# A pruned matmul's opening: the hand-written order of its first products, transposes and pruning steps

## Chip, cores and metric

The kernel runs on one core of one Trainium2 chip. The metric is the device time of one execution in microseconds (us). The engines of the core are TensorE (PE in the profile; PEld is its weight load), VectorE (DVE), ScalarE (ACT), GpSimd (POOL) and SyncE (SP), which issues DMAs. Every time below is from a run, the page of one profiled execution, or an answer of its trace.

## The reference

x is 16 x 512 rows of 1024 numbers, w is 1024 x 1024, b has 1024, all bf16. In every column of w, each four consecutive rows form a group, and the two smaller of the four by absolute value are set to zero; then the product and the bias follow.

```
wg = w.reshape(G, M, D)                 # M = 4, G = 256
mag = jnp.abs(wg)
thr = the third of the four magnitudes in ascending order
mask = mag >= thr
wp = (wg * mask).reshape(D, D)
out = einsum("bsd,df->bsf", x, wp) + b
```

## The kernel before, in words

The 8192 rows of x are 64 token tiles of 128. TensorE multiplies a transposed tile of x (128 x 128, loaded as weights) by a stretch of the pruned weights wp, up to 512 columns wide, into a PSUM bank. For nearly the whole run (`nat`, line 241, products on line 243) it uses wp_nat, the pruned weights in the natural order of rows, and tiles of x that a DMA has transposed; there are eight products per tile and half of the columns.

**The opening** is there because at the start neither the pruned weights nor transposed tiles exist. w comes in six *pieces* (line 135): pieces 0 to 3 are 256 columns each of the first half of the rows (group block g = 0), pieces 4 and 5 are 512 columns each of the second half. Seven tiles of x (0 to 6), called packed, are loaded as they are, transposed on TensorE against an identity (`transpose`, line 194, four transposes a tile into one bank) and copied to SBUF by ScalarE (`copy_xt`, line 202). In w as loaded, each partition holds a whole group of four rows: these four *rows* are named u, v, s and t (slices 0 to 3; line 209), x is u and v, y is s and t. With them a product needs no rearranged weights: TensorE can start on a piece's row as soon as VectorE has pruned it. Seven tiles, four pieces and four rows give 112 products of 256 columns (`mm_piece`, line 215; the product is on line 229).

**Pruning a piece** (`Piece.do`, line 169) is a chain on VectorE: abs; hi and lo (maximum and minimum of the pairs); t1 and t2 (minimum of the his, maximum of the los); thr; mask; mult, which writes wp. thr and all in front of it work on all four rows, mask and mult may be cut by rows. Piece 0 has its abs cut in two (a, b), since its two halves arrive by two DMAs.

**The sums of the opening.** PSUM has eight banks for this kernel: two in the pool psum_t, for transposed tiles, and six in psum_o, for sums (lines 60 and 61). A sum takes a bank of 512 columns for two tiles and one piece (the pairs are tiles 3 and 4, 0 and 1, 2 and 5) or, for tile 6 alone, for two pieces. Tile 4 is transposed into a bank of psum_o, and the fillers write to one. When all products of a sum are done, ScalarE copies it out (`stage`, line 260) and its bank comes free for the next tile that asks.

**The orders.** What each engine does in the opening, and in which order, is written out by hand in the table `order` from line 267 on, one list of tokens for each engine; an engine takes its list strictly in order. `needs` (line 305) only says when a token may be written into the program, `emit` (line 345) writes it; the waits come from the data. Tokens:

- T5a: transpose tile 5. C5a: its copy on ScalarE. F4: four filler products of 128 columns on constants (line 143), which compute nothing.
- M5.0t: products of tile 5, piece 0, row t. x and y stand for two products.
- hi0, mask0t, mult0t and so on: steps of pruning piece 0; abs3 in ScalarE's list is the abs of piece 3.
- S3b0: copy out the sum of pair 3 and piece 0 (pair 0 is tiles 3 and 4, pair 2 is 0 and 1, pair 3 is 2 and 5). U6h0: the same for tile 6, first half of the columns.
- W0.0: DMAs (four, on SyncE; W1.0q on ScalarE) that spread the pruned weights of block 0, columns 0 to 511, from wp to wp_nat. Z, X1, Y0, Y1: further loads.
- E0, A0h0 and so on: first products from wp_nat. E0 is the first of them.

Ahead of the lists stand 6 fillers of 512 columns and 14 of 128. After the lists come the closing products of the first twelve tiles, and then seven batches of tiles with eight products for each half of the columns. Bias additions on the way out are on VectorE (lines 428 and 430).

Of the kernel before, what the change touches and what calls it, by code (L numbers as in the profile page):

```python
# [10 lines left out]
def kernel(  # L11
# [8 lines left out]
    P = 128  # L20
    bf16 = mybir.dt.bfloat16
    fp32 = mybir.dt.float32
# [10 lines left out]
    FH = 512  # L33
# [26 lines left out]
    psum_t = ctx.enter_context(tc.tile_pool(name="psum_t", bufs=2, space=bass.MemoryType.PSUM))  # L60
    psum_o = ctx.enter_context(tc.tile_pool(name="psum_o", bufs=6, space=bass.MemoryType.PSUM))
# [10 lines left out]
    def pe(i):  # L72
        return seq("pe", i)
# [7 lines left out]
    def sp(i):  # L81
        return seq("sp", i)
# [19 lines left out]
    def load_w(g, c0, c1, ma=0, mb=4, eng="sp"):  # L102
        issue(eng, w_sb[:, g, ma:mb, c0:c1], wv[:, g, ma:mb, c0:c1])
# [10 lines left out]
    def load_lead(g):  # L114
        t0 = NPK - g
        sp(nc.sync.dma_start_transpose(out=xlead[:, 4 * g:4 * g + 4, (t0 - SOLO) * P:],
                                       in_=xf[t0 * P:(NPK + LEAD) * P, g * HK:(g + 1) * HK]))
        return {t: xlead[:, :, (t - SOLO) * P:(t - SOLO + 1) * P] for t in range(t0, NPK + LEAD)}
# [22 lines left out]
    def filler(n, rep=1):  # L141
        for _ in range(n):
            pe(nc.tensor.matmul(warm_ps[:, :rep * P], lhsT=nc.const_aps.tensor(1.0, [P, P], bf16),  # L143
                                rhs=nc.const_aps.tensor(1.0, [P, rep * P], bf16), start=True, stop=True))
# [4 lines left out]
    def spread(g, c0, c1, ks=range(4), eng="sp"):  # L149
        for k in ks:  # L150
            issue(eng, wp_nat[:, 4 * g + k, c0:c1], wp[32 * k:32 * k + 32, g, :, c0:c1])
# [38 lines left out]
                self.tt(wp[:, self.g, ms, self.c0:self.c1], self.w[:, ms, :], self.mag[:, ms, :], Alu.mult)  # L190

    xpk = {}

    def transpose(t):
        xg = x_sb[t].rearrange("p (q m) -> p m q", m=4)
        bank = psum_o.tile([P, FH], fp32, name="ps") if t == 4 else psum_t.tile([P, FH], fp32, name="tp")
        tp = bank[:].bitcast(bf16)[:, :FH].rearrange("p (m q) -> p m q", m=4)
        for m in range(4):
            pe(nc.tensor.transpose(tp[:, m, :], xg[:, m, :], ident[:]))  # L199
        xpk[t] = tp  # L200
# [33 lines left out]
    def load_low(u):  # L234
        a, b_ = GROUPS[u]
        xlow = const.tile([P, 4, (b_ - a) * P], bf16, name=f"xlow{u}")
        sp(nc.sync.dma_start_transpose(out=xlow[:], in_=xf[a * P:b_ * P, HK:]))
        xq = xlow[:].rearrange("p k (q t) -> p k q t", t=b_ - a)
        return {a + t: xq[:, :, :, t] for t in range(b_ - a)}
# [20 lines left out]
    def stage(key):  # L260
        solo = key[1] == "h"
        q, h, at = (pair_of[key[0]], key[2], int(key[0] != SOLO)) if solo else (key[0], key[1] // 2, key[1] % 2)
        if (q, h) not in staged:
# [2 lines left out]

    order = {
# [7 lines left out]
        ),  # L275
        "dve": (
# [4 lines left out]
        ),  # L281
        "act": (
            "C5a C3a C4a C6a C2a C0a C1a S3b0 S2b0 abs3 S0b0 U6h0 S3b1 S0b1 S2b1 S3b2 S0b2 S2b2 S2b3 S0b3 U6h1 "
            "S3b3 U7h0 W1.0q U7h1"
        ),
        "sp": (
            "W0.0 Z W0.1 X1 W1.0p Y1 Y0 W1.1"
# [1 line left out]
    }  # L289
    written = {"X0"}  # L290
    p = {}
    halves = {0: tuple("uvst"), 1: ('x', 'y'), 2: ('u', 'v', 'y'), 3: ('x', 'y')}

    by_rows = {0}

    def all_of(tok, i):
        return [tok + x for x in halves.get(i, ("",))]

    def split_tok(tok):
        k = tok[-1] if tok[-1] in "xyabuvst" else ""  # L300
        return (tok[:-1] if k else tok), k

    transposed = []

    def needs(eng, tok):
        base, k = split_tok(tok)
        if tok[0] == "C":
            return ["T" + tok[1:]]
        if tok[0] == "T":
            return ["C" + transposed[-2]] if tok != "T4a" and len(transposed) > 1 else []  # L310
        if tok[0] == "F":
            return []
        if tok[0] == "W":
            g, h = map(int, tok[1:4].split("."))
            return [n for i, pc in enumerate(pieces) if pc[0] == g and pc[1] // FH == h for n in all_of(f"mult{i}", i)]
        if tok[0] in "XYZ":
            return []
        if tok[0] == "A":
            return ["X0", f"W0.{tok.split('h')[1]}"] + ([f"U{NPK}h{tok[-1]}"] if tok[1] == "3" else [])
        if tok[0] == "E":  # L320
            return ["X0", f"W0.{tok[1]}"]
        if tok[0] == "U":
            t, h = map(int, tok[1:].split("h"))
            if t == NPK:
                return [f"E{h}"]
            return [f"M{t}.{x}" for i, pc in enumerate(pieces) if pc[0] == 0 and pc[1] // FH == h for x in all_of(str(i), i)]
        if base[0] == "M":
            t, i = base[1:].split(".")
            return [f"C{t}a", f"mult{i}{k}"]
        if tok[0] == "S":  # L330
            q, n = map(int, tok[1:].split("b"))
            return [f"M{t}.{x}" for i, pc in enumerate(pieces) if pc[0] == 0 and pc[1] // CW == n
                    for t in pairs[q] for x in all_of(str(i), i)]
        i, step = base[-1], base[:-1]
        before = {"abs": [], "hi": ["abs"], "lo": ["abs"], "t1": ["hi"], "t2": ["lo"],
                  "thr": ["t1", "t2"], "mask": ["thr", "hi", "lo"], "mult": ["mask"]}[step]
        out_ = []
        for b_ in before:
            if b_ in ("abs", "hi", "lo") and int(i) in by_rows:
                out_ += [b_ + i + k] if step in ("hi", "lo") else [b_ + i + s for s in "ab"]  # L340
            else:
                out_.append(b_ + i + (k if b_ == "mask" else ""))
        return out_

    def emit(eng, tok):
        base, k = split_tok(tok)
        if tok[0] == "T":
            transpose(int(tok[1:-1]))
            if tok != "T4a":
                transposed.append(tok[1:])  # L350
        elif tok[0] == "F":
            filler(int(tok[1:]))
        elif tok[0] == "W":
            g, h = map(int, tok[1:4].split("."))
            spread(g, h * FH, (h + 1) * FH, {"": range(4), "p": range(2), "q": range(2, 4)}[tok[4:]], eng)
        elif tok[0] == "Z":
            load_w(1, 512, 1024)
            sp(nc.sync.dma_start(bias_sb[:], b.partition_broadcast(P)))
        elif tok[0] == "X":
            xnat.update(load_lead(int(tok[1:])))  # L360
        elif tok[0] == "Y":
            xnat.update(load_low(int(tok[1:])))
        elif tok[0] == "E":
            open_solo(int(tok[1:]))
        elif tok[0] == "U":
            t, h = map(int, tok[1:].split("h"))
            stage((t, "h", h))
        elif tok[0] == "A":
            open_nat(*map(int, tok[1:].split("h")))
        elif tok[0] == "C":  # L370
            copy_xt(int(tok[1:-1]))
        elif tok[0] == "M":
            mm_piece(*map(int, base[1:].split(".")), part[k])
        elif tok[0] == "S":
            stage(tuple(map(int, tok[1:].split("b"))))
        else:
            i = int(base[-1])
            if i not in p:
                p[i] = Piece(i)
            if eng == "act":  # L380
                p[i].abs_act()
            else:
                p[i].do(base[:-1], part[k], half.get(k, slice(0, 2)))
# [82 lines left out]
    for bi, (tb, nb) in enumerate(batches):  # L466
        if bi:
            load_batch(bi + 1)
        for j in range(nb):
            t = tb + j  # L470
            xt = xnat[t]
            o = outp.tile([P, Dout], bf16, name="o")
            if t == NT - 1:
                for n, (c0, c1) in enumerate(((0, FH), (FH, FH + CW), (FH + CW, Dout - P), (Dout - P, Dout))):
                    ps = psum_o.tile([P, FH], fp32, name="ps")
# [44 lines left out]
```

## Time and profile before

| what | value |
|---|---|
| median of the runs | 233.09 us (3 runs, 232.59 to 233.63) |
| span of the profiled execution, first to last instruction | 232.0 us |
| TensorE busy | 226.2 us, 98% of the span, 1128 products and transposes |
| VectorE busy | 107.9 us (47%) |
| ScalarE busy | 13.3 us (6%) |
| bytes moved by the DMA engines | 38.19 MB, mean 165 GB/s over the span |
| small products of the opening (line 229) | 112, 273 ns each by the profile |
| transposes (line 199) | 28 |
| fillers (line 143) | 24 |

The runs were timed apart from the profile; the profiled execution's own time is its span and what lies around it, and the span is 1.1 us under the median of the runs. A row of a timeline gives start, length, engine, line, operation, output <- input, shape and a count of merged instructions, and in brackets how long the engine sat idle ahead of it and for whom. Products on TensorE are pipelined: the length of one is longer than the distance to the next, so distances are read from the starts.

### The profile page before, as it was taken

Reading aid. Unit: us, or ns where it says so; the run is one execution under the profiler, and the core shown is the slowest. Engines: PE = TensorE matmul, PEld = TensorE weight load, DVE = VectorE, ACT = ScalarE, POOL = GpSimd, SP = SyncE. Lnnn points to the kernel's source line nnn. Section 1 sums busy time; section 2 is a strip of 40 time slices with the busy share of each in tenths; the row PEclk is TensorE's granted clock in tenths of the full one; section 3 lists DMA queues with packets and bytes.
Section 4 is the critical chain, followed back from the end, with each engine's and each line's share of the span. In section 5 each row is a group of like instructions: output and inputs, shape, how many; then the busy total and the mean of one; then the engine's idle time right before and its main releaser. Section 6 shows DMA issues by size and latency. Waiting matters only on the chain.

```text
span 232.0 us, 2815 instructions
## 1 busy us (share of the span) xinstructions
PE 226.2 (98%) x1128; PEld 110.4 (48%) x1148; DVE 107.9 (47%) x194; ACT 13.3 (6%) x26; POOL 17.6 (8%) x15
## 2 busy tenths in 40 slices
PE   7899999999999999999999999999999999999995
PEld 4786444444444444444444444444444444444443
DVE  4899967754234334334324324424424423423434
ACT  2576100000000000000000000000000000000000
POOL 1000099800000000000000000000000000000000
PEclk9999999999999999999999999999999999999999
DMA  6999999997299321991239721797229952122122
GB/s 201 255 193 266 261 182 230 277 312 271 95 206 259 123 93 54 261 273 45 93 103 275 210 90 51 146 240 212 81 90 184 241 163 77 61 90 90 48 90 90
DMA packets 79292, 38.19 MB, mean 165 GB/s; under 512 B 64176, under 2 KB 71728, under 8 KB 79280
## 3 DMA queue, kind: packets, MB, share of 16 engines
q1 hardware_dynamic: 68352, 20.75, 43.5%
q10 hardware_dynamic: 10928, 17.27, 21.1%
q8 instruction: 9, 0.15, 0.3%
q14 instruction: 3, 0.02, 0.0%
HBM read 3.28 MB, written 16.78 MB: 86 GB/s over the span
## 4 chain that ended last, share of the span: by engine, by line
PE 96%; DMA 2%; issue 1%; ACTq 0%; DVE 0%
PE ps L243 87%; PE ps L229 5%; PE tp L243 2%; DMA x<-in_x_dram 2%; PE tp L199 1%; ACTq L100 0%; DVE o L428 0%; PE ps L143 0%
## 5 line engine op out<-in xcount | busy, mean ns | idle before, releaser
L243 PE MATMUL ps<-wp_nat,xb 128*128 128x512 bf16 (+1 forms) x831 | 178.9, 375 | 0.9
L243 PEld LDWEIGHTS <-xb 128*128 128x128 bf16 x848 | 82.4, 98 | 97.5
L428 DVE TENSOR_TENSOR o<-ps,bias_sb 128x512 bf16<-128x512 f32 (+1 forms) x112 | 71.6, 677 | 113.8 <-PE ps L243 111.5
L424 POOL TENSOR_TENSOR st<-st,bias_sb 128x1024 f32<-128x1024 f32 x8 | 16.7, 2124 | 0.0
L243 PE MATMUL ps<-wp_nat,xlead 128*128 128x512 bf16 x63 | 14.7, 379 | 0.1
L243 PEld LDWEIGHTS <-xlead 128*128 128x128 bf16 x88 | 8.6, 98 | 10.2
L229 PE MATMUL ps<-wp,xt 128*128 128x256 bf16 x112 | 12.9, 273 | 0.0
L430 DVE TENSOR_TENSOR o<-ps,st 128x512 bf16<-128x512 f32 x16 | 11.1, 692 | 2.8 <-PE ps L243 2.2
L229 PEld LDWEIGHTS <-xt 128*128 128x128 bf16 x112 | 10.8, 98 | 1.2
L243 PE MATMUL ps<-wp_nat,xlow 128*128 128x512 bf16 x47 | 10.6, 379 | 0.1
L265 ACT COPY st<-ps 128x512 f32<-128x512 f32 x14 | 7.4, 594 | 3.0 <-PE ps L229 3.0
L243 PEld LDWEIGHTS <-xlow 128*128 128x128 bf16 x48 | 5.0, 103 | 5.4
L164 DVE TENSOR_TENSOR wp<-w_sb,mag 128x256 bf16<-128x256 bf16 (+2 forms) x13 | 6.2, 482 | 0.1
L164 DVE TENSOR_TENSOR mag<-mag,hi 128x256 bf16<-128x256 bf16 (+2 forms) x13 | 6.0, 482 | 0.2
L243 PE MATMUL tp<-wp_nat,xlead 128*128 128x512 bf16 x23 | 5.8, 379 | 0.0
L143 PE MATMUL ps<-const-bfloat16-1.0 128*128 128x128 bf16 (+1 forms) x24 | 4.1, 334 | 0.8 <-PEq L504 0.8
L174 DVE TENSOR_SCALAR mag<-w_sb 128x512 uint16<-128x512 uint16 (+2 forms) x6 | 2.7, 468 | 4.2 <-DMA w_sb<-in_w_dram 4.2
L199 PE MATMUL tp<-ident,x 128*128 128x128 bf16 x24 | 2.2, 224 | 1.3 <-DMA x<-in_x_dram 1.3
L143 PEld LDWEIGHTS <-const-bfloat16-1.0 128*128 128x128 bf16 x24 | 2.1, 118 | 2.4 <-issue 2.4
L164 DVE TENSOR_TENSOR hi<-mag 128x512 bf16<-128x512 bf16 (+2 forms) x7 | 3.2, 456 | 0.0
L164 DVE TENSOR_TENSOR lo<-mag 128x512 bf16<-128x512 bf16 (+2 forms) x7 | 3.1, 457 | 0.0
L199 PEld LDWEIGHTS <-x 128*128 128x128 bf16 x28 | 1.8, 115 | 2.0 <-DMA x<-in_x_dram 2.0
(18 smaller groups left out, 15.0 us busy)
## 6 DMA issues: line engine op xcount, KB each, us to landing
out_dram<-o ACTq DMA_DIRECT2D x58, 256.0 KB, 2.4
wp_nat<-wp SPq DMA_DIRECT2D x14, 128.0 KB, 3.3
out_dram<-o ACTq DMA_DIRECT2D x10, 128.0 KB, 1.7
w_sb<-in_w_dram SPq DMA_DIRECT2D x2, 512.0 KB, 5.3
w_sb<-in_w_dram SPq DMA_DIRECT2D x3, 256.0 KB, 5.9
x<-in_x_dram SPq DMA_DIRECT2D x2, 256.0 KB, 4.7
x<-in_x_dram ACTq DMA_DIRECT2D x2, 128.0 KB, 4.3
bias_sb<-in_b_dram SPq DMA_DIRECT2D x1, 256.0 KB, 4.7
```

What stands on the lines that cost most here:

```text
L143: pe(nc.tensor.matmul(warm_ps[:, :rep * P], lhsT=nc.const_aps.tensor(1.0, [P, P], bf16), rhs=nc.const_aps.tensor(1.0, [P, rep * P], bf16), ...
L164: dve(nc.vector.tensor_tensor(out, a, b_, op=op))
L174: dve(nc.vector.tensor_single_scalar(self.mag[:, ms, :].bitcast(u16), self.w[:, ms, :].bitcast(u16), 0x7FFF, op=Alu.bitwise_and))
L199: pe(nc.tensor.transpose(tp[:, m, :], xg[:, m, :], ident[:]))
L229: pe(nc.tensor.matmul(ps[:, c0 + d:c1 + d], lhsT=xpk[t][:, m, :], rhs=wp[:, g, m, c0:c1], start=(new and m == ms.start), stop=(left[key] = ...
L243: pe(nc.tensor.matmul(ps, lhsT=xt[:, kt - koff, :], rhs=wp_nat[:, kt, c0:c1], start=(kt == first), stop=(kt == last)))
L265: act(nc.scalar.copy(staged[(q, h)][:, at, :, :].rearrange("p t c -> p (t c)"), ps_open.pop(key)[:]))
L424: pool(nc.gpsimd.tensor_tensor(st[:], st[:], bias.to_broadcast([P, 2, 2, CW]), op=Alu.add))
L428: dve(nc.vector.tensor_tensor(o[:, c0:c1], ps, bias_sb[:, c0:c1], op=Alu.add))
L430: dve(nc.vector.tensor_tensor(o[:, c0:c1].rearrange("p (n c) -> p n c", n=2), ps.rearrange("p (n c) -> p n c", n=2), add, op=Alu.add))
```

## The change

Only the tables of the opening change, and the few lines that know their names.

- **TensorE.** T6a moves behind the products M5.0t and M5.0s. The fillers F4 are gone. Each tile then runs its rows of piece 0 together (t, s, then u, v), and of the other pieces all seven tiles run one row before the next: t, s, x for piece 1, with the tiles in the order 3, 4, 6, 5, 2, 0, 1.
- **Tile 1** is transposed into a bank of psum_o, as tile 4 was (OWN).
- **VectorE.** hi0 and lo0 run over all four rows at once (512 columns) instead of in halves, lo first. mask0v and mult0v move ahead of abs1, as does mult0u. Piece 1 is masked as t, s, x instead of y, x. abs2 leaves its list.
- **ScalarE.** abs2 joins its list, ahead of the first copy of a sum (S0b0, then S3b0, S2b0, abs3); the later copies come in the order of the new products.
- SyncE's list is unchanged.

```diff
+    OWN = (4, 1)
...
-        bank = psum_o.tile([P, FH], fp32, name="ps") if t == 4 else psum_t.tile([P, FH], fp32, name="tp")
+        bank = psum_o.tile([P, FH], fp32, name="ps") if t in OWN else psum_t.tile([P, FH], fp32, name="tp")
...
         "pe": (
-            "T5a T3a T4a T6a F4 M5.0t M3.0t M5.0s M3.0s M4.0t M4.0s T2a M6.0s M3.0u M6.0u M5.0u T0a M4.0u T1a "
-            "M2.0s M2.0t M2.0u M6.0t M0.0u M0.0s M0.0t M1.0t M0.0v M2.0v M1.0v M5.0v M6.0v M3.0v M4.0v M1.0u "
-            "M1.0s M2.1y M3.1y M5.1y M2.1x M6.1y M0.1x M1.1x M4.1x M6.1x M5.1x M0.1y M4.1y M3.1x M1.1y M2.2y "
-            "M3.2y M1.2y M6.2y M4.2y M4.2v M5.2y M5.2v M1.2v M2.2u M0.2v M0.2y M4.2u M0.2u M5.2u M6.2v M2.2v "
-            "M3.2u M1.2u M6.3x M0.3x M5.3x M3.2v M3.3x M1.3y M4.3y M1.3x M0.3y M4.3x M3.3y M6.3y M6.2u M2.3y "
-            "M2.3x M5.3y E0 A0h0 A2h0 A1h0 A3h0 E1 A2h1 A0h1 A1h1 A3h1"
+            "T5a T3a T4a M5.0t M5.0s T6a M3.0t M3.0s M4.0t M4.0s M6.0t M6.0s M5.0u M5.0v M3.0u M3.0v T2a M4.0u "
+            "M4.0v M6.0u M6.0v T0a T1a M2.0t M2.0s M2.0u M2.0v M0.0t M0.0s M0.0u M0.0v M1.0t M1.0s M1.0u M1.0v "
+            "M3.1t M4.1t M6.1t M5.1t M2.1t M0.1t M1.1t M3.1s M4.1s M6.1s M5.1s M2.1s M0.1s M1.1s M3.1x M4.1x "
+            "M6.1x M5.1x M2.1x M0.1x M1.1x M3.2y M4.2y M6.2y M5.2y M2.2y M0.2y M1.2y M3.2v M4.2v M6.2v M5.2v "
+            "M2.2v M0.2v M1.2v M3.2u M4.2u M6.2u M5.2u M2.2u M0.2u M1.2u M3.3x M4.3x M6.3x M5.3x M2.3x M0.3x "
+            "M1.3x M3.3y M4.3y M6.3y M5.3y M2.3y M0.3y M1.3y E0 A0h0 A2h0 A1h0 A3h0 E1 A2h1 A0h1 A1h1 A3h1"
         ),
         "dve": (
-            "abs0a abs0b hi0a lo0a lo0b hi0b t20 t10 thr0 mask0t mask0s mult0t mult0s mask0u abs1 mult0u hi1 lo1 "
-            "t11 t21 mask0v thr1 mult0v mask1y mask1x mult1y abs2 mult1x lo2 hi2 t22 t12 thr2 mask2y mask2v "
-            "mult2y mask2u mult2v hi3 lo3 t13 t23 mult2u thr3 mask3x mult3x mask3y mult3y abs4 hi4 lo4 t24 t14 "
-            "thr4 mask4 mult4 abs5 lo5 hi5 t25 t15 thr5 mask5 mult5"
+            "abs0a abs0b lo0 hi0 t20 t10 thr0 mask0t mask0s mult0t mult0s mask0u mask0v mult0u mult0v abs1 hi1 "
+            "lo1 t11 t21 thr1 mask1t mask1s mult1t mask1x mult1s mult1x lo2 hi2 t22 t12 thr2 mask2y mask2v mult2y "
+            "mask2u mult2v hi3 lo3 t13 t23 mult2u thr3 mask3x mult3x mask3y mult3y abs4 hi4 lo4 t24 t14 thr4 "
+            "mask4 mult4 abs5 lo5 hi5 t25 t15 thr5 mask5 mult5"
         ),
         "act": (
-            "C5a C3a C4a C6a C2a C0a C1a S3b0 S2b0 abs3 S0b0 U6h0 S3b1 S0b1 S2b1 S3b2 S0b2 S2b2 S2b3 S0b3 U6h1 "
-            "S3b3 U7h0 W1.0q U7h1"
+            "C5a C3a C4a C6a C2a C0a C1a abs2 S0b0 S3b0 S2b0 abs3 S0b1 U6h0 S3b1 S2b1 S0b2 S3b2 S2b2 S0b3 U6h1 "
+            "S3b3 S2b3 U7h0 W1.0q U7h1"
...
-    halves = {0: tuple("uvst"), 1: ('x', 'y'), 2: ('u', 'v', 'y'), 3: ('x', 'y')}
+    halves = {0: tuple("uvst"), 1: ('s', 't', 'x'), 2: ('u', 'v', 'y'), 3: ('x', 'y')}
...
-            return ["C" + transposed[-2]] if tok != "T4a" and len(transposed) > 1 else []
+            return ["C" + transposed[-2]] if int(tok[1:-1]) not in OWN and len(transposed) > 1 else []
...
-            if b_ in ("abs", "hi", "lo") and int(i) in by_rows:
-                out_ += [b_ + i + k] if step in ("hi", "lo") else [b_ + i + s for s in "ab"]
+            if b_ == "abs" and int(i) in by_rows:
+                out_ += [b_ + i + s for s in "ab"]
...
-            if tok != "T4a":
+            if int(tok[1:-1]) not in OWN:
```

## The prediction

> **What bounds the kernel now.** I read the page's chain first, then the list of waits, then the timeline of the opening engine by engine. The first fence has the page's span, its chain by engine and by line, and the costliest group; the second the list of TensorE's waits from 6.6 us to the end.
>
> ```profile
> span 232.0 us, 2815 instructions
> ...
> PE 96%; DMA 2%; issue 1%; ACTq 0%; DVE 0%
> PE ps L243 87%; PE ps L229 5%; PE tp L243 2%; DMA x<-in_x_dram 2%; PE tp L199 1%; ACTq L100 0%; DVE o L428 0%; PE ps L143 0%
> ...
> L243 PE MATMUL ps<-wp_nat,xb 128*128 128x512 bf16 (+1 forms) x831 | 178.9, 375 | 0.9
> ```
> ```profile
> PE tp L199 <- DMA x<-in_x_dram: 0.6, 1, 0.6
> ```
>
> The chain is TensorE for 96% of the span. The one listed wait of TensorE is for x at 6.6 us, the very start of that stretch; after it TensorE is fed to the end. So the change can only act where its order differs: from the first transpose to E0, the first product that reads the pruned weights from wp_nat. What E0 gains or loses there moves the end by the same amount, as long as later data keep their lead. The opening on TensorE:
>
> ```profile
> 5.57 0.39 PE L199 MATMUL ps<-ident,x 128*128 128x128 bf16 x4
> 6.60 0.41 PE L199 MATMUL tp<-ident,x 128*128 128x128 bf16 x4 [0.64 <-DMA x<-in_x_dram]
> 6.85 0.39 PE L143 MATMUL ps<-const-bfloat16-1.0 128*128 128x128 bf16 x4
> 7.08 0.82 PE L229 MATMUL ps<-wp,xt 128*128 128x256 bf16 x6
> 7.81 0.41 PE L199 MATMUL tp<-ident,x 128*128 128x128 bf16 x4
> 8.07 0.60 PE L229 MATMUL ps<-wp,xt 128*128 128x256 bf16 x4
> 8.59 0.42 PE L199 MATMUL tp<-ident,x 128*128 128x128 bf16 x4
> 8.85 0.27 PE L229 MATMUL ps<-wp,xt 128*128 128x256 bf16 x1
> 8.96 0.39 PE L199 MATMUL tp<-ident,x 128*128 128x128 bf16 x4
> 9.18 11.19 PE L229 MATMUL ps<-wp,xt 128*128 128x256 bf16 x101
> 20.20 1.03 PE L243 MATMUL tp<-wp_nat,xlead 128*128 128x512 bf16 x4
> ```
>
> The rows are start, length, engine, line. T4's transposes end at 5.57 + 0.39 = 5.96, T6 starts at 6.60 when its x lands, F4 (four fillers) takes 6.85 to 7.08, and the last 101 of the 112 small products run from 9.18 to E0 at 20.20: 11.02 / 101 = 0.109 us each, with no gap. A transposed tile costs 0.22 (8.96 to 9.18), and 0.26 where TensorE had to wait (7.81 to 8.07), so a restart costs 0.04.
>
> **The change part by part.** First VectorE, whose rows set when weights are ready:
>
> ```profile
> 3.31 0.51 DVE L174 TENSOR_SCALAR mag<-w_sb 128x512 uint16<-128x512 uint16 x2 [3.31 <-DMA w_sb<-in_w_dram]
> ...
> 4.54 0.28 DVE L164 TENSOR_TENSOR lo<-lo 128x256 bf16<-128x256 bf16 x1
> 4.75 0.28 DVE L164 TENSOR_TENSOR hi<-hi 128x256 bf16<-128x256 bf16 x1
> 5.07 0.29 DVE L164 TENSOR_TENSOR hi<-hi,lo 128x256 bf16<-128x256 bf16 x1
> 5.39 0.49 DVE L164 TENSOR_TENSOR mag<-mag,hi 128x256 bf16<-128x256 bf16 x2
> 5.80 0.49 DVE L164 TENSOR_TENSOR wp<-w_sb,mag 128x256 bf16<-128x256 bf16 x2
> ...
> 7.43 0.43 DVE L174 TENSOR_SCALAR mag<-w_sb 128x1024 uint16<-128x1024 uint16 x1 [0.94 <-DMA w_sb<-in_w_dram]
> ...
> 7.97 0.42 DVE L164 TENSOR_TENSOR hi<-mag 128x512 bf16<-128x512 bf16 x1
> 8.31 0.42 DVE L164 TENSOR_TENSOR lo<-mag 128x512 bf16<-128x512 bf16 x1
> ...
> 11.33 0.42 DVE L164 TENSOR_TENSOR lo<-mag 128x512 bf16<-128x512 bf16 x1
> ...
> 13.39 0.42 DVE L164 TENSOR_TENSOR wp<-w_sb,mag 128x512 bf16<-128x512 bf16 x1
> ...
> 16.18 0.43 DVE L164 TENSOR_TENSOR wp<-w_sb,mag 128x512 bf16<-128x512 bf16 x1
> ```
>
> Independent steps follow each other after 0.20 (256 wide, 4.54 to 4.75) or 0.34 (512 wide, 7.97 to 8.31); a dependent one starts 0.03 after its source ends (5.07 + 0.29 = 5.36, next 5.39).
>
> *Wider first steps.* Four steps of 0.20 become two of 0.34, 0.12 less. But lo0 needs both halves of abs0, which end at 3.31 + 0.51 = 3.82: lo0 3.86, hi0 4.20, t20 4.54, t10 waits for hi0 (4.62) and starts at 4.73, thr0 5.04, mask0t 5.36 against 5.39. So the wait eats nearly all: 0.03 is left. mult0t ends at about 6.06, mult0s at 6.26, mult0u and mult0v by 7.07, all before the DMA of piece 1 lets abs1 start at 7.43.
>
> *Tile 5 ahead of tile 6.* M5.0t starts 0.04 after mult0t (the lag of the copy behind T6: 6.60 + 0.41 = 7.01, copy at 7.05 in the next fence), at 6.10; M5.0s at 6.30, done at 6.41, before x of tile 6 is there. Two products leave the bound stretch: 2 x 0.109 = **-0.22**. Cover gone (mult0s over 0.19 later), it costs one for one.
>
> *No F4*: 7.08 - 6.85 = **-0.23**. *T2 and T0* each waited shortly for x: 7.08 + 6 x 0.109 = 7.73 against 7.81, and 8.07 + 0.44 = 8.51 against 8.59, each with a restart: 2 x (0.08 + 0.04), or **-0.23** before rounding. Below they come later than their data.
>
> *M6.0t.* With F4 gone, M3 and M4 (four products) run 6.85 to 7.29, but tile 6's copy ends at 7.42. ScalarE's rows:
>
> ```profile
> 7.05 0.37 ACT L204 COPY xt<-tp 128x256 f32<-128x256 f32 x1 [0.57 <-PE tp L199]
> ...
> 9.05 0.70 ACT L204 COPY xt<-tp 128x256 f32<-128x256 f32 x2 [0.41 <-PE tp L199]
> 10.69 1.13 ACT L265 COPY st<-ps 128x512 f32<-128x512 f32 x2 [0.94 <-PE ps L229]
> 11.72 1.06 ACT L167 ACTIVATE mag<-w_sb 128x1024 bf16<-128x1024 bf16 x1
> 12.68 2.09 ACT L265 COPY st<-ps 128x512 f32<-128x512 f32 x4
> ```
>
> M6.0t starts at 7.46: a new wait of 0.17 and a restart, **+0.21**; all behind it on TensorE waits too. Then six products to 8.16 (restart counted), T2 to 8.38, four products to 8.82, T0 to 9.04, T1 to 9.26 (with its own bank of psum_o it no longer waits for the copy of tile 2), twelve products to 10.57. Piece 1's t row: abs1 ends 7.86, hi1 7.89, lo1 8.23, t21 8.77, thr1 9.08, mask1t 9.40, mult1t about 9.81 to 10.09. In time, by 0.48.
>
> *The bank wait.* In the new order the sums of piece 1 open while those of piece 0 are all open: tiles 2/5, 3/4, 6 and 0/1 hold four of psum_o's six banks, M3.1t and M5.1t take the other two. M0.1t, the sixth product of piece 1, due at 10.57 + 5 x 0.109 = 11.11, needs a seventh. It must wait for the first staging copy, S0b0, and abs2 now stands ahead of that on ScalarE. Tile 0's copy starts 0.04 after T0 ends (8.82 + 0.39 = 9.21), at 9.25; tile 1's 0.33 later (0.70 - 0.37) at 9.58, abs2 at 9.91, S0b0 0.96 later (11.72 to 12.68) at 10.87, and with the 0.59 of such a copy (1.13 for two that start 0.54 apart) it ends at 11.46. M0.1t starts at 11.50: 0.39 and a restart, **+0.43**. Behind it on TensorE stand all other products, E0 among them; ScalarE's later copies wait for those products, VectorE doesn't. The trace of before shows no wait for a bank. Its ends: nothing, if a bank came free otherwise; 1.5, if the bank given were that of the third copy (2 x 0.54 later). I take 0.43, since six open sums can be counted and ScalarE's rows are at hand.
>
> The other 79 products follow: 11.54 + 79 x 0.109 = 20.15 for E0, against 20.20. As a sum: -0.22 - 0.23 - 0.23 + 0.21 + 0.43 = **-0.04**.
>
> *abs2 moved to ScalarE, the fixed row order, the rest of VectorE.* abs2 leaves VectorE (0.34) and ends at 10.97; lo2 starts at about 11.01 instead of 11.33. So everything behind is about 0.32 early: piece 2's first weights end at 13.81 - 0.32 = 13.49, needed when 56 products are left (20.15 - 6.10 = 14.05); piece 3's at 16.61 - 0.32 = 16.29, needed at 14.05 + 28 x 0.109 = 17.10. The later banks have slack of about 0.4 or more by the same spacing. These edits cost nothing while these leads of 0.5 and 0.8 last; beyond them, one for one.
>
> *DMAs and queues.* No moved step issues a DMA, and SyncE's list is the same. Its rows, and one issue alone, that of piece 2 of the weights, with its time to landing at the end:
>
> ```profile
> w_sb<-in_w_dram SPq DMA_DIRECT2D x1, 256.0 KB, 5.9
> ```
> ```profile
> 3.59 2.02 SPq L100 DMA_DIRECT2D w_sb<-in_w_dram  x3
> 5.65 6.19 SPq L116 DMA_TRANSPOSE xlead<-in_x_dram  x1
> 11.96 3.42 SPq L100 DMA_DIRECT2D wp_nat<-wp  x4
> ```
>
> The spread of the first half (W0.0) goes out right behind the long transposing load, at 11.96, whether piece 1 is done at 11.4 or 11.0: no gain, no loss. All later transfers are asked for at the same time or earlier.
>
> So E0 moves by -0.04 us, the span to 231.96, and the median, 1.1 above the span of the profiled execution, from 233.09 to **233.05**. The end of the time outside the span has no row, and I leave it as it is.
>
> **The rivals.**
>
> *No new waits* (12%): if S0b0 is through in time (abs2 short, or another bank free), the 0.43 goes: 232.6; with M6.0t's 0.21 too, 232.4, the most that the edits can bring (0.68). For it: ScalarE stood idle 0.94 before 10.69. Against it: in the new order abs2 fills just that idle time.
>
> *The staging queue tied to a DMA* (slower, 8%): abs2 waits for piece 2 of the weights, and S0b0, so M0.1t, stands behind it. Issued at 3.59, landed 5.9 later, at 9.5, against abs2's turn at 9.91. From a landing after 9.9 on, each 0.1 us later is 0.1 us on TensorE; at 11.1 (7.5 us to landing) the time is 234.3. Against it: 5.9 here, and no row of before shows piece 2 late. With a bank that comes with the third copy, 1.1 more on TensorE, the time is 234.1 (5%).
>
> *The clock* (slower, 2%): the fillers are what keeps TensorE's clock up, and F4 goes. The first two rows are weight loads of the wide fillers at the start; the third is the stretch 6.60 to 9.18 with its granted clock in the third column from the end.
>
> ```profile
> 1.58 0.15 PEld L143 LDWEIGHTS <-const-bfloat16-1.0 128*128 128x128 bf16 x1 [0.27 <-issue]
> 2.01 0.15 PEld L143 LDWEIGHTS <-const-bfloat16-1.0 128*128 128x128 bf16 x1 [0.28 <-issue]
> 6.60:9.18 2.58, 2.58 (x32) 2.11 (x32) 1.75 (x7) 0.88 (x3) 0.00 (x0) 1.00 1.12 318
> ```
>
> A wide filler took 0.43 (1.58 to 2.01) at first, where 512-wide products later take 178.9 / 831 = 0.215: half pace. Each us at half pace costs 0.5; it decides from 2.4 us on, and 3 us of it would give 234.5. In before the stretch holds 1.00, and in the new order TensorE's idle time before 6.60 gets shorter, not longer. The Trainium skill (TensorE: Matmul & The Clock Gate, "Part 4: PE-mode transpose") says that transposes do not count as busy for the gate, which speaks against dropping F4. Its Part 1 wants a whole idle window of about 3.4 us; the trace agrees so far, in that the clock held at 1.00.
>
> **How the numbers follow.** About 0.5% (1.17 us) is what a measurement of this kernel can tell from no change. Forecast with its small errors 67%; no new waits 12%; the DMA case 8%, half of it under 0.5%; third copy's bank 5%, just within 0.5%; clock 2%; what I have not seen 6%, half to each side. The forecast's bounds are 232.4 (all gains, no wait) and about 233.9 (some leads of 0.4 to 0.5 lost); with the scatter of the runs of before, 232.59 to 233.63, the range is 232.3 to 234.0. Faster by over 0.5% needs more than the whole 0.68 and gets half of the unseen, 3%; slower gets half of the DMA case, the clock and the other half of the unseen, 4 + 2 + 3 = 9%; within, 88%.
>
> **What would show it.** Right: two 256-wide products before T6's transposes; a TensorE gap of about 0.2 after four products behind T6, and one of about 0.4 at the 34th small product, ended by a ScalarE copy; E0 near 20.15; mask0t near 5.36. Wrong: no such gap (232.6), a gap of over a microsecond, a wait of TensorE behind E0, or products farther apart than 0.109.

## The result and the profile after

The changed kernel takes 233.45 us (median of 22 runs, 233.32 to 233.65), the kernel before 233.03 (22 runs, 232.59 to 233.74): a ratio of 1.0018, 95% interval 1.0012 to 1.0025. That is 0.42 us slower, inside the predicted range and inside 0.5%, but with the other sign than the forecast of -0.04. And the changed kernel scatters by 0.33 us, the kernel before by 1.15.

The page of the changed kernel: its span, and its chain by engine and by line (lines are one higher than before).

```profile
span 231.5 us, 2828 instructions
...
PE 95%; DVE 1%; DMA 1%; ACT 1%; issue 0%
PE ps L244 88%; PE ps L230 5%; PE tp L244 2%; DMA w_sb<-in_w_dram 1%; ACT mag L167 0%; DVE hi L164 0%; PE tp L200 0%; ACT xt L205 0%; DVE lo L164 0%; DVE mag L174 0%; DVE mag L164 0%; ACT st L266 0%; DVE o L429 0%; DVE wp L164 0%
```

Two things are to be seen. The chain no longer begins with x of tile 6: it begins with the first load of w, runs through VectorE's first steps (hi, lo, mag, wp) and later through ScalarE (xt, mag, st). And the span of this execution is shorter than that of before (231.5 against 232.0), although the kernel is slower. This execution took 233.33 in all, so 1.8 us lie around the span. The profiled execution of before, at a span of 232.0, then took about 233.8: 0.8 above its own median. The prediction had read an execution from the upper end of the scatter. E0 gives the same: in 14 of the 17 profiled executions whose own time is known, the time is E0 plus 213.57 to 213.61 us (in the other three plus 213.69 to 213.81), and 20.20 + 213.6 is 233.8.

TensorE's opening in the changed kernel, as in the prediction's fence of before:

```profile
5.35 0.39 PE L200 MATMUL ps<-ident,x 128*128 128x128 bf16 x4
6.10 0.47 PE L230 MATMUL ps<-wp,xt 128*128 128x256 bf16 x2 [0.37 <-DVE wp L164]
6.41 0.38 PE L200 MATMUL tp<-ident,x 128*128 128x128 bf16 x4
6.63 1.46 PE L230 MATMUL ps<-wp,xt 128*128 128x256 bf16 x10
7.93 0.39 PE L200 MATMUL tp<-ident,x 128*128 128x128 bf16 x4
8.15 0.60 PE L230 MATMUL ps<-wp,xt 128*128 128x256 bf16 x4
8.59 0.39 PE L200 MATMUL tp<-ident,x 128*128 128x128 bf16 x4
8.81 0.39 PE L200 MATMUL ps<-ident,x 128*128 128x128 bf16 x4
9.03 10.89 PE L230 MATMUL ps<-wp,xt 128*128 128x256 bf16 x96
19.76 1.03 PE L244 MATMUL tp<-wp_nat,xlead 128*128 128x512 bf16 x4
```

T6 starts at 6.41 and waits for no DMA; it stands behind M5.0t and M5.0s, which wait for VectorE, with TensorE idle before 6.10. How early its x was there is in the DMA view of that one issue, whose last number is the time to landing, first in the changed kernel, then in the execution of before that the prediction read:

```profile
x<-in_x_dram ACTq DMA_DIRECT2D x1, 128.0 KB, 3.6
```
```profile
x<-in_x_dram ACTq DMA_DIRECT2D x1, 128.0 KB, 4.8
```

Issued at 1.8 in both, it landed at 5.4 here and at 6.6 there. T6 needs one thing more, the bank of tile 5, which is free when tile 5's copy ends (in two runs below, in which T6 does not wait for its own x, it starts 0.05 behind that copy: 5.91 behind 5.86, 5.92 behind 5.87). Here that copy runs from 5.32 to 5.69. So T6 could have started at about 5.7, in time in which TensorE now does nothing.

The two waits that the prediction added are both there. The chain of the changed kernel, start, length, what:

```profile
6.79 0.44 PE ps L230 x4
...
7.26 0.83 PE ps L230 x6
...
9.01 0.65 ACT xt L205 x2
9.66 0.96 ACT mag L167
10.61 0.48 ACT st L266
11.10 0.04 issue
11.14 8.78 PE ps L230 x79
```

M6.0t starts at 7.26 instead of 6.63 + 4 x 0.109 = 7.07, 0.19 late. The last 79 products hang on tile 1's copy, abs2 and S0b0 on ScalarE, as forecast, and begin at 11.14. The row of 96 in the timeline takes 19.76 - 9.03 = 10.73, where 96 x 0.109 is 10.47: the bank wait is 0.25.

### The profile page after: what moved, and what is told of

Its sections match the earlier page's. It is cut to its first block, busy times and chain, and to the rows that moved or that the text cites. A ratio compares the mean times of both kernels' runs of the same rounds, so it can differ in the third digit from the quotient of the medians.

```text
span 231.5 us, 2828 instructions
## 1 busy us (share of the span) xinstructions
PE 227.6 (98%) x1144; PEld 110.7 (48%) x1144; DVE 107.9 (47%) x193; ACT 13.8 (6%) x27; POOL 17.6 (8%) x15
## 3 DMA queue, kind: packets, MB, share of 16 engines
HBM read 3.28 MB, written 16.78 MB: 87 GB/s over the span
## 4 chain that ended last, share of the span: by engine, by line
PE 95%; DVE 1%; DMA 1%; ACT 1%; issue 0%
PE ps L244 88%; PE ps L230 5%; PE tp L244 2%; DMA w_sb<-in_w_dram 1%; ACT mag L167 0%; DVE hi L164 0%; PE tp L200 0%; ACT xt L205 0%; DVE lo L164 0%; DVE mag L174 0%; DVE mag L164 0%; ACT st L266 0%; DVE o L429 0%; DVE wp L164 0%
## 5 line engine op out<-in xcount | busy, mean ns | idle before, releaser
L244 PE MATMUL ps<-wp_nat,xb 128*128 128x512 bf16 (+2 forms) x848 | 179.8, 375 | 0.0
L164 DVE TENSOR_TENSOR lo<-mag 128x512 bf16<-128x512 bf16 (+1 forms) x6 | 3.1, 510 | 0.2
L164 DVE TENSOR_TENSOR hi<-mag 128x512 bf16<-128x512 bf16 (+1 forms) x6 | 3.1, 509 | 0.1
L167 ACT ACTIVATE mag<-w_sb 128x1024 bf16<-128x1024 bf16 x2 | 2.2, 1086 | 0.0
```

The lines of the kernel that those rows point to most:

```text
L164: dve(nc.vector.tensor_tensor(out, a, b_, op=op))
L167: act(nc.scalar.activation(self.mag[:], self.w, Act.Abs))
L244: pe(nc.tensor.matmul(ps, lhsT=xt[:, kt - koff, :], rhs=wp_nat[:, kt, c0:c1], start=(kt == first), stop=(kt == last)))
```

## Experiments

The ratios are to the kernel before on the same chip. Where kernels ran on one chip, they are also compared with each other. *x ready* names the kernels in which tiles 6, 2, 0 and 1 are transposed from the data of tiles 5 and 3. Where a kernel's E0 is given, it is from its profile.

### T6 ahead again

```diff
-T4a M5.0t M5.0s T6a M3.0t
+T4a T6a M5.0t M5.0s M3.0t
```

> The changed kernel with one thing undone: T6 stands ahead of M5.0t and M5.0s again (F4 stays away, the bank wait stays). Theory (x of tile 6 usually lands early, at about 5.4 us as in the profile after, so the transposes of tile 6 were work in TensorE's idle time before 6.1 and the change moves them behind it): T6 starts at about 5.6, its 0.22 and the 0.19 wait of M6.0t go, E0 comes 0.41 earlier, at about 19.35; median about 233.0, ratio to before about 1.000. Rival (the bank wait alone makes it slower): no change from the changed kernel, 1.0018.

Measured: 233.14, before 233.33, ratio 0.9996 (0.9984 to 1.0008). The changed kernel's excess is gone within that interval. T6 at 5.6 and E0 at 19.35, which were expected, did not come in the profiled execution (6.17 and 19.77). It shows no wait at M6.0t, the bank wait stays at 0.25, and E0 is late for another reason: TensorE's first transposes ran at half pace, T6's among them (see the last section).

### abs2 back on VectorE

```diff
-mask1x mult1s mult1x lo2          (VectorE)
+mask1x mult1s abs2 mult1x lo2
-C1a abs2 S0b0                     (ScalarE)
+C1a S0b0
```

> The changed kernel with abs2 back on VectorE, between mult1s and mult1x, and out of ScalarE's list. Theory (the bank wait at M0.1t, 0.25 in the profile after, is one of two losses): the wait at the 34th small product goes, E0 0.25 earlier; median about 233.2, ratio about 1.0007, as long as VectorE, 0.15 later at lo2, stays ahead of the products of piece 2. Rival (the bank wait is all): ratio 1.000 or below. Rival (VectorE is the next limit): no gain, a new wait for VectorE at the first product of piece 2.

Measured: 233.25, ratio 0.9995 (0.9984 to 1.0007). TensorE's last small products in this kernel:

```profile
9.08 10.64 PE L230 MATMUL ps<-wp,xt 128*128 128x256 bf16 x96
19.56 1.03 PE L244 MATMUL tp<-wp_nat,xlead 128*128 128x512 bf16 x4
```

19.56 - 9.08 = 10.48 for the 96: the bank wait is gone, and no wait for VectorE has come in its place. The time is where it was expected (233.2), but the ratio alone would fit the rival that the bank wait is all (1.000 or below; 1.0007 was expected). The kernel before stands at 233.33 on this chip, on the others at 233.03 to 233.18, and a change of 0.2 is within that; the next series, on one chip, separates the two losses.

### Parts of the change alone, in the kernel before

```diff
-T4a T6a F4 M5.0t M3.0t M5.0s M3.0s     (b_t6_behind)
+T4a M5.0t M5.0s T6a F4 M3.0t M3.0s
-T6a F4 M5.0t                           (b_no_f4)
+T6a M5.0t
```

> The kernel before with one part of the change: M5.0t and M5.0s ahead of T6, F4 kept behind T6. Theory (x early): T6 and F4, which cost nothing in the idle time before 6.1, now cost 0.22 and 0.23, and M5.0s waits 0.09 for mult0s: about 0.5 slower where x is early, 0.2 faster where x is late; median about 233.4, ratio 1.001 to 1.002. The prediction's account (x late, as in the profile before): 0.22 faster, ratio 0.999.

> The kernel before without the four fillers F4. Theory (x early): F4 runs in the idle time before the first product, so nothing is gained; ratio 0.9995 to 1.000. The prediction's account: 0.23 faster, ratio 0.999. Clock rival: slower, with products farther apart than 0.109 us.

Measured: with T6 behind 233.36, ratio 1.0004 (0.9992 to 1.0015); without F4 233.04, ratio 0.9988 (0.9974 to 1.0002). The first fell between its two accounts, the second leans to the prediction's. Against a kernel that scatters by over 1 us, neither settles anything. In the profile without F4, T6 waits for its x until 6.08 and the first product follows at 6.35: there F4 would have stood on the path.

### x ready

```diff
-xg = x_sb[t].rearrange(...)
+xg = x_sb[5 if t == 6 else min(max(t, 3), 5)].rearrange(...)
```

> The kernel before, but the transposes of tiles 6, 2, 0 and 1 read tiles 5 and 3 instead of their own data (their own loads are still issued), so that no transpose but the first waits for a late x; the outputs of these four tiles are those of other rows. Theory (when x is early, T6 and F4 fit into TensorE's idle time before the first product at 6.1): no wait but the first products' start; E0 at about 6.1 + 112 x 0.109 + 0.66 = 19.0; median about 232.6 and little scatter, ratio 0.997. Rival (landing of x has nothing to do with it): as before.

> The changed kernel with the same replacement of x. Theory: unchanged from the changed kernel, since its T6 waits for mult0s and not for x; E0 19.8, median about 233.4, so 0.7 to 0.8 slower than the kernel before with x ready. Rival (landing of x has nothing to do with it): 0.4 slower than that one, as the two kernels themselves.

> The changed kernel with x ready and T6 ahead of M5.0t and M5.0s again. Theory: 0.41 faster than the changed kernel with x ready (T6's 0.22 and M6.0t's wait of 0.19 go), the bank wait of 0.25 stays: about 233.0. Rival (the bank wait is all): no gain.

> The changed kernel with x ready and abs2 back on VectorE. Theory: the bank wait goes, 0.25 faster than the changed kernel with x ready: about 233.15; the waits at M5.0s (0.09) and M6.0t (0.19) stay. Rival (VectorE is the next limit): no gain, a wait for VectorE at the first product of piece 2.

Measured on one chip (before 233.04): before with x ready 233.30 (232.72 to 234.04); changed 233.54 (233.37 to 233.79); changed with T6 ahead 233.11 (11 of 12 runs 233.01 to 233.28); changed with abs2 on VectorE 233.32 (233.09 to 233.44). So within the changed kernel T6's place is worth 0.43 (0.41 expected) and the bank wait 0.22 (0.25 expected). The first expectation failed: with x ready the kernel before did not go to 232.6, and still scattered by 1.3 us. So did the gap of 0.7 to 0.8 that the second expected: it is 0.24, and its rival's 0.4 did not come either. Late x is not the only thing that holds it. Its profile shows another one:

```profile
4.78 1.06 PE L199 MATMUL tp<-ident,x 128*128 128x128 bf16 x8
5.63 0.63 PE L199 MATMUL ps<-ident,x 128*128 128x128 bf16 x4
6.06 0.52 PE L199 MATMUL tp<-ident,x 128*128 128x128 bf16 x4
6.42 0.39 PE L143 MATMUL ps<-const-bfloat16-1.0 128*128 128x128 bf16 x4
6.65 0.82 PE L229 MATMUL ps<-wp,xt 128*128 128x256 bf16 x6
```

The first eight transposes take 0.85 from start to start of the next row, 0.106 each; in the changed kernel's profile a transposed tile later takes 0.22, 0.055 each. At half pace T6 and F4 no longer fit ahead of the first product, which starts at 6.65.

### x late, a try that did not delay it

```diff
-load_x(SOLO, SOLO + 1, "act")
 act(nc.scalar.activation(spark[:], ...))
+load_x(SOLO, SOLO + 1, "act")
```

> The kernel before with x of tile 6 loaded about 2 us later (its DMA is issued behind the first activation on ScalarE, about 3.8 instead of 1.8 us), so that T6 surely waits. Theory: T6 at about 8.0, then F4 and all 112 products behind it: E0 about 21.4, median about 235.0.

> The changed kernel with x of tile 6 loaded just as late. Theory (the sign of the change hangs on when x lands): now two products run in the wait for x and no F4 behind it, against the waits at M6.0t and for the bank: 0 to 0.2 slower than the kernel before with the late load, where the two kernels themselves differ by 0.4. Rival (the waits it adds are all that counts): 0.4 or more slower than that one.

The load was still issued ahead of the activation, at 1.85 instead of 1.78, so x was not late, and both expectations fell with that. The two are in effect the plain kernels again: 233.14 (ratio 0.9991, 0.9970 to 1.0013) and 233.49 (1.0015, 1.0003 to 1.0026). The first one's profiled execution took 233.18, close to that kernel's median, and serves below as a typical execution of the kernel before:

```profile
5.99 0.41 PE L199 MATMUL tp<-ident,x 128*128 128x128 bf16 x4 [0.27 <-ACT xt L204]
6.24 0.39 PE L143 MATMUL ps<-const-bfloat16-1.0 128*128 128x128 bf16 x4
6.47 0.82 PE L229 MATMUL ps<-wp,xt 128*128 128x256 bf16 x6
7.20 0.41 PE L199 MATMUL tp<-ident,x 128*128 128x128 bf16 x4
7.45 0.60 PE L229 MATMUL ps<-wp,xt 128*128 128x256 bf16 x4
7.99 0.41 PE L199 MATMUL tp<-ident,x 128*128 128x128 bf16 x4
...
19.60 1.03 PE L243 MATMUL tp<-wp_nat,xlead 128*128 128x512 bf16 x4
```

T6 starts at 5.99, not 6.60, and everything up to E0 is 0.60 earlier than in the execution that the prediction read. The row names tile 5's copy as the last that T6 waited for, but that copy ended at 5.68; T6's own x, issued at 1.85, landed 4.1 us later, at 5.95.

### The kernel before once more

> The kernel before, unchanged, to see another of its executions. Theory (the profile that the prediction read was an execution with late loads): x of tile 6 lands at 5.4 to 6.3 us instead of 6.55, T6 starts before 6.3, E0 stands at 19.0 to 19.6 instead of 20.20, and the time is 232.6 to 233.2. Rival (that profile was typical, and the time is lost elsewhere): E0 at 20.1 to 20.3 again.

Measured: 233.09 (232.68 to 233.76). Its profiled execution took 233.60: T6 at 6.33, E0 at 20.00. Neither account's numbers are met in full: T6 is earlier than 6.60, but the time lies in the upper part of the scatter. It shows that E0 of the kernel before moves from execution to execution: 19.60 in the fence above, 20.00 here, 20.20 in the one that the prediction read.

### x late

```diff
-load_x(SOLO, SOLO + 1, "act")
...
 load_x(0, 2)
+load_x(SOLO, SOLO + 1)
```

> The kernel before with the load of tile 6 moved from ScalarE's queue to SyncE's, behind the loads of tiles 2, 0 and 1, so that its x lands at about 8.2 us and T6 surely waits. Theory: T6 at about 8.3, then F4 and all 112 products behind it without a wait: E0 about 21.7, median about 235.3.

> The changed kernel with the same late load of tile 6. Theory (the sign and size of the change hang on when x of tile 6 lands): against the kernel before with the same load the two products ahead of T6 and the absence of F4 bring the 0.45 that the prediction gave them, the waits at M6.0t (0.19) and for the bank (0.27) cost the same, and T2 and T0 wait in neither: 0.0, at most 0.1 either way. Rival (the order is worse whatever x does): 0.4 slower, as for the two kernels themselves.

Measured: before with x late 236.03 (6 runs, 234.81 to 236.36), ratio 1.0113 (1.0093 to 1.0134); changed with x late 234.80 (6 runs, 234.41 to 236.40), ratio 1.0083 (1.0057 to 1.0110). By the medians the changed kernel is now the faster one (the intervals overlap), but that can't be put down to the order. Four of the six runs of before (235.95 to 236.36) and two of the six of the changed kernel (235.87 and 236.40) have a mean granted clock of 0.992 or 0.993, the others 1.000; 0.7% of 234 us is 1.6 us, an estimate of what that is worth. At 1.000 stand 234.81 and 235.68 against 234.41 to 234.89, too few for a verdict. What remains are the two profiled executions, both at 1.000 (235.68 and 234.59). The first fence is of the kernel before, the second of the changed one:

```profile
8.70 0.41 PE L199 MATMUL tp<-ident,x 128*128 128x128 bf16 x4 [2.77 <-DMA x<-in_x_dram]
...
22.07 1.03 PE L243 MATMUL tp<-wp_nat,xlead 128*128 128x512 bf16 x4
```
```profile
7.63 0.42 PE L200 MATMUL tp<-ident,x 128*128 128x128 bf16 x4 [1.06 <-DMA x<-in_x_dram]
...
21.01 1.03 PE L244 MATMUL tp<-wp_nat,xlead 128*128 128x512 bf16 x4
```

From T6 to E0 the first takes 22.07 - 8.70 = 13.37, the second 21.01 - 7.63 = 13.38: 0.0, as expected. What the two orders gain and lose cancels once T6 waits for its x. Of the 1.09 between these two executions, 1.07 is the landing of x itself (T6 at 8.70 and at 7.63): the load goes out at 3.6 in both and takes 5.1 and 4.0 us. Why it differs, and why the granted clock is lower in half of the runs, stays open: no profile is of a run at the lower clock. Of all other runs with a clock on record only two, of the kernel before (235.61 and 235.90), show it.

### F4 and mult0 with x ready

```diff
-T6a F4 M5.0t                                   (b_x_ready_no_f4)
+T6a M5.0t
-mask0u abs1 mult0u hi1 lo1 t11 t21 mask0v thr1 mult0v    (b_x_ready_mult0)
+mask0u mask0v mult0u mult0v abs1 hi1 lo1 t11 t21 thr1
```

> The kernel before with x ready (the transposes of tiles 6, 2, 0 and 1 read tiles 5 and 3, so these four tiles' outputs are those of other rows) and without F4. Theory of the clock (the time at which TensorE's pace doubles differs from 3.6 to 6.7 us from execution to execution, and F4 at half pace no longer fits ahead of the first product): 0.2 to 0.3 under the kernel before with x ready, about 233.0. Rival (mult0u, behind abs1, waits for piece 1 of the weights): no gain.

> The kernel before with x ready in the same way, F4 kept, and mask0v, mult0u and mult0v ahead of abs1 on VectorE. Theory of the clock: no gain on the kernel before with x ready (233.3 there). Rival (mult0u waits behind abs1 for piece 1 of the weights): the upper half of its runs, 233.4 to 234.0, disappears, about 233.0.

Measured: without F4 233.04 (232.67 to 233.71), ratio 0.9992 (0.9978 to 1.0005); with mult0 ahead 233.31 (232.91 to 233.80), ratio 0.9999 (0.9988 to 1.0010). Beside 233.30 with both left alone (on another chip, ratio 1.0001), the numbers came out as the theory of the clock has it, but the intervals overlap, and the profiles do not bear it out. The first fence is of the kernel without F4, the second of the one with mult0 ahead:

```profile
6.96 0.39 PE L199 MATMUL tp<-ident,x 128*128 128x128 bf16 x4
7.19 0.27 PE L229 MATMUL ps<-wp,xt 128*128 128x256 bf16 x1
7.66 0.49 PE L229 MATMUL ps<-wp,xt 128*128 128x256 bf16 x3 [0.20 <-DVE wp L164]
```
```profile
8.24 2.02 PE L229 MATMUL ps<-wp,xt 128*128 128x256 bf16 x17
10.66 9.38 PE L229 MATMUL ps<-wp,xt 128*128 128x256 bf16 x84 [0.39 <-DVE wp L164]
```

Without F4, M3.0u waits for mult0u, 7.66 instead of 7.19 + 0.109 = 7.30: the rival is at work. With mult0 ahead that wait is gone, but the 29th product, M2.1y, the first of piece 1, now waits for VectorE, 10.66 instead of 8.24 + 17 x 0.109 = 10.09. The edit brought a loss of its own, so its missing gain says nothing against the rival. F4, x and mult0u take turns as the last to be ready; I can't give each its share of the scatter.

### Both losses undone

```diff
-T4a M5.0t M5.0s T6a M3.0t
+T4a T6a M5.0t M5.0s M3.0t
-M3.1t M4.1t M6.1t M5.1t M2.1t M0.1t M1.1t M3.1s M4.1s M6.1s M5.1s M2.1s M0.1s M1.1s
+M3.1t M4.1t M6.1t M5.1t M2.1t M3.1s M4.1s M6.1s M5.1s M2.1s M0.1t M1.1t M0.1s M1.1s
```

> The changed kernel with T6 ahead of M5.0t, and with the t and s rows of piece 1 done first for tiles 3, 4, 6, 5, 2 and only then for 0 and 1, so that the sum that needs a seventh bank opens five products later, behind S0b0. Theory (both losses are these two): E0 0.41 + 0.25 before the 19.76 of the changed kernel, 19.1; median 232.7 to 232.9, faster than both kernels, ratio 0.998 to 0.999. Rival (VectorE is the next limit): a wait at the first product of piece 2, and about 233.0.

Measured: 232.99 (232.73 to 233.55), ratio 0.9994 (0.9980 to 1.0008); on the same chip the changed kernel (with its load moved by 0.06 us, in the try that did not delay x) took 233.49. Its rows:

```profile
5.01 1.04 PE L200 MATMUL tp<-ident,x 128*128 128x128 bf16 x8
5.84 0.43 PE L200 MATMUL ps<-ident,x 128*128 128x128 bf16 x4
6.11 0.39 PE L200 MATMUL tp<-ident,x 128*128 128x128 bf16 x4
6.33 1.56 PE L230 MATMUL ps<-wp,xt 128*128 128x256 bf16 x12
...
8.83 10.64 PE L230 MATMUL ps<-wp,xt 128*128 128x256 bf16 x96
19.31 1.03 PE L244 MATMUL tp<-wp_nat,xlead 128*128 128x512 bf16 x4
```

96 products in 10.48: no bank wait, with abs2 still on ScalarE; and no wait for VectorE at piece 2. From the first product to E0 it takes 19.31 - 6.33 = 12.98, the changed kernel 19.76 - 6.10 = 13.66: 0.68 less, where 0.41 + 0.25 were expected. But the first product comes 0.23 later, since the first eight transposes ran at half pace (5.01 to 5.84) and T6 stands ahead of it, so E0 at 19.1 and 232.7 to 232.9 were missed. The kernel takes back what the change lost (0.50), and cannot be told from the kernel before.

## Why the prediction was wrong, step by step

**VectorE's first steps: right.** In the changed kernel mask0t starts at 5.35 (forecast 5.36) and M5.0t at 6.10, as forecast:

```profile
3.83 0.42 DVE L164 TENSOR_TENSOR lo<-mag 128x512 bf16<-128x512 bf16 x1
...
5.35 0.49 DVE L164 TENSOR_TENSOR mag<-mag,hi 128x256 bf16<-128x256 bf16 x2
```

lo0 waits for abs0b (forecast 3.86). From the first step to mask0t it is 5.35 - 3.28 = 2.07, before 5.39 - 3.31 = 2.08: the wider steps bring 0.01 (forecast 0.03).

**The terms**, as forecast, and as they stand between the typical execution of before (233.18) and the profiled one of the changed kernel (233.33):

| term | forecast | measured | from |
|---|---|---|---|
| two products ahead of T6, and no F4 | -0.45 | -0.06 | third product of piece 0 at 6.63, against 6.47 + 2 x 0.109 = 6.69 |
| waits and restarts of T2 and T0 | -0.23 | -0.24 | before: T2 at 7.20 for 7.12, T0 at 7.99 for 7.89, 0.03 each to restart; after: none |
| M6.0t waits for tile 6's copy | +0.21 | +0.19 | 7.26 for 7.07 |
| M0.1t waits for a bank | +0.43 | +0.25 | 96 products in 10.73 for 10.48 |
| sum | -0.04 | +0.14 | E0 at 19.60 and 19.76: +0.16 |

**The step that failed is the first term, and in it the place of T6.** It held T6 at 6.60 in both kernels, waiting for its x, so that two products could run in that wait and F4 behind it could go. That held in the execution that was read. In the typical one T6 starts at 5.99, ahead of about 6.1, where mult0t lets the first product start. So M5.0t and M5.0s fill no wait for x: they push T6 from 5.99 to 6.41. These 0.42, less the 0.03 of a restart, take back 0.39 of the 0.45; the two products (0.22) and F4 (6.24 to 6.47, 0.23) did bring what was forecast. With x at 5.4, as in the changed kernel's own execution, all of T6 would have fitted between 5.7 and 6.10. The size of the term hangs on one landing. The pair with x late gives the forecast's case (13.37 and 13.38 from T6 to E0), and the changed kernel with T6 ahead, x ready, shows the price of the other (0.43).

At the medians even less is left of the gains. With the 213.6 us between E0 and the time, the medians stand for E0 at about 19.45 and 19.87 (an estimate; no profile fell there). The two new waits, 0.19 and 0.25, make 0.44, as much as the whole 0.42: of the 0.68 that the first two terms were to bring, nothing is to be seen.

**The bank wait: right in mechanism, too large.** Tile 1's copy, now from a bank of psum_o, followed tile 0's by less than the 0.33 taken, and abs2 followed that one as closely:

```profile
9.01 0.37 ACT L205 COPY xt<-tp 128x256 f32<-128x256 f32 x1 [0.29 <-PE tp L200]
9.28 0.38 ACT L205 COPY xt<-ps 128x256 f32<-128x256 f32 x1
9.54 1.07 ACT L167 ACTIVATE mag<-w_sb 128x1024 bf16<-128x1024 bf16 x1
10.50 1.56 ACT L266 COPY st<-ps 128x512 f32<-128x512 f32 x3
```

0.27 and 0.26 instead of 2 x 0.33: 0.13 of the missing 0.18. The restart of 0.04 that the forecast put on top does not show either (11.14 + 79 x 0.109 = 19.75, E0 at 19.76).

**From the profile to the median: wrong.** The prediction took the 1.1 between the span and the median for time around the span and carried the sum over. That time is 1.8 (233.33 against 231.5; also 235.68 against 233.9 in the kernel before with x late), so the profiled execution lay 0.8 above the median, and its T6, at 6.60, stands later than in the two other executions of that order (6.33 at 233.60, 5.99 at 233.18). How the measured 0.42 goes with the table: this typical execution lies 0.15 above the median of the kernel before, the changed kernel's 0.12 under its own, and 0.15 is the difference of the two. What makes up the first two is not known.

**The rivals.** No wait that the forecast did not name appeared in the changed kernel, and abs2 was never late for its weights. Its products ran 0.109 apart after F4 was gone (79 from 11.14 to 19.76); a slower pace stands in the profiles only between the first two products of the kernel with T6 ahead (about 0.15), behind transposes that were still at half pace. The Trainium skill (TensorE: Matmul & The Clock Gate, "Part 4: PE-mode transpose") says that transposes do not count as busy for the gate; no run here shows a loss from it. The clock of 1.00 that the prediction took as a sign is none: the column shows it at half pace too (last section). The case that came, T6 ready to start before the first product, was not among the rivals.

**The scatter.** In the changed kernel T6 and all behind it hang on VectorE, and so on the first load of w. In three executions of that order (as it is, with x ready, with the load moved by 0.06) VectorE's first step starts at 3.28, 3.45 and 3.55, E0 stands at 19.76, 19.91 and 20.02, and the times are 233.33, 233.49 and 233.60, in nearly the same steps. The changed kernel and its four variants with T6 behind M5.0s and x not late (two with x ready, abs2 on VectorE, the load moved) scatter by 0.33 to 0.55, the three with T6 ahead by 0.82 to 1.05. That the rest (x, the pace of the first transposes) falls into TensorE's idle time before 6.10 I only argue from the chains of the profiles; no run holds each of them fixed.

## What to carry to other kernels

A wait read in one execution is one draw: hold the profiled execution's own time against the spread of the runs, and if it lies at the edge, size every wait for a DMA from both ends. A step that stands in front of a wait on another engine may be free; moving it behind that wait makes it cost its full length. And an order that opens sums row by row needs more banks at once: count the open sums, and look at what now stands ahead of the copy that frees the first.

## What the runs showed of the hardware

- The same load of 128 KB, issued at the same time, took between 3.6 and 4.8 us to land, by the two DMA rows above.
- A mean granted clock of 0.992 or 0.993 in place of 1.000 went with 235.6 to 236.4 us in eight runs, six of them with x late.
- TensorE's pace doubled at a time that differed between executions. In the changed kernel with T6 ahead T6's four transposes still took 0.41 (6.17 to 6.58, first fence), in the typical execution of before, earlier in time, 0.25 (5.99 to 6.24) with a restart in it. The granted clock of the views did not show this pace: the second fence, of the changed kernel as it is, has 1.00 (third column from the end) for 0.80 to 3.30 us, where wide fillers run 0.43 apart as in the kernel before (0.215 later in the run). So the distance of equal products is the better witness.

```profile
6.17 0.61 PE L200 MATMUL tp<-ident,x 128*128 128x128 bf16 x4
6.58 1.52 PE L230 MATMUL ps<-wp,xt 128*128 128x256 bf16 x12
```
```profile
0.80:3.30 2.50, 2.50 (x7) 0.83 (x8) 0.02 (x1) 1.03 (x1) 0.43 (x2) 1.00 0.53 157
```
